# First block of a fused light convolution and feed-forward kernel: convolution work moved among TensorE, VectorE and GpSimd

## Chip, core and metric

One core of a Trainium2 chip runs the whole kernel. The metric is the time of one execution on the device in microseconds (us); for a kernel several runs are taken and their median is compared. All tensors are float32.

## What is computed

The input x has 8 sequences of 4096 tokens with 192 channels. A causal convolution comes first: for each of 8 heads (24 channels each) seven weights are put through a softmax, and each channel of a token is the weighted sum of that channel in this token and the six before it. Then a feed-forward layer follows:

```
w = softmax(weight, over the 7 taps)                # 8 heads x 7
y[t, c] = sum over k of w[head(c), k] * x[t - 6 + k, c]   # zero before a sequence
h = y @ w_in                                        # 192 -> 2048
g = h if h >= 1, 0 if h <= -1, else (h + 1)^2 / 4
out = g @ w_out                                     # 2048 -> 192
```

## The kernel before, in words

The 32768 tokens are cut into 64 blocks of 512. A block has 8 steps, one for each pair of 128-wide tiles of the 2048 hidden features; there are 512 steps, numbered q. In step q TensorE computes the hidden tiles (`mm1`, L351) and then the output matmuls of step q - 2 (`mm2_first`, L373, in the first two blocks; `mm2`, L395, after). Other engines turn h into g in between. Two PSUM buffers hold h, so `mm1` of step q + 2 needs h of step q to be read.

Block 0 runs `mm1` in plain float32: 6 products a step, each against halves of 64 partitions. From block 1 on, weights and activations are split into a rounded part and what is left, and `mm1` makes 18 matmuls of the faster rounded type (float32r). Its operands come in the order n (channels as they lie), s (halves swapped by DMA) and r (the channels from 128).

The order of the work on each engine is written out by hand; an engine takes its instructions in the order of the program, and each waits on what it needs.

Two blocks form a chunk of tokens, A and B. A unit of convolution is `a` (channels 0 to 127 of A), `b` (the same of B) or `r` (channels 128 to 191 of A and of B, one below the other). A unit is loaded in pieces of 32 channels and transposed by VectorE (`transpose`, L131), or, at the start, loaded with tokens on the partitions (`load_plain`, L101) and transposed by TensorE (`transpose_pe`, L133). Its seven taps are multiplied and summed on VectorE (`taps_dve`, L178), on ScalarE and GpSimd (`taps`, L188: ScalarE multiplies, GpSimd adds, L196 and L197), or by TensorE with diagonal matrices (`taps_pe`, L152). `split` (L206) makes the rounded part on ScalarE and the rest of it on VectorE or GpSimd, and swaps the halves of both by four DMAs of the SP queue (L202, L203).

The weights w_in and w_out come in ten chunks as pairs of words. ScalarE scales both words (`floats`, L286: m and r), VectorE puts them together (`bits`, L297: L304, L306 and L311 or L313). Later ScalarE rounds them (`hi`, L328) and VectorE makes the rest (`lo`, L332); the tables `PARTS` (L643) say in which step.

The start (L531 to L610): a few matmuls on dummy data, the loads on SP, the softmax of the weights, a matmul (`spread`, L578) that hands each channel its weights. Unit a takes taps 4 to 6 on VectorE and 0 to 3 on TensorE; unit r takes all seven on VectorE. Then the words of chunks 0, 1 and half of 2 are turned, and step 0 can begin.

`first_step` (L659) is the work of ScalarE and VectorE in steps 0 to 7: relu and square on ScalarE (L669, L675), the maximum on VectorE (L679), the words of chunk q + 3, the taps of unit b on VectorE by the table `FIRST_B` (L619), and in step 6 the split of unit b, ahead of the square. `conv_slot` (L623) starts the units of the next chunk. `evac_last` (L477) adds the output sums of the last block, transposes them with matmuls (L497) and stores them.

Of the kernel before, what the change touches and what calls it, by code (L numbers as in the profile page):

```python
# [30 lines left out]
def lightconv_then_ffn(ctx: ExitStack, tc: tile.TileContext, x, weight, w_in, w_out, out):  # L31
# [52 lines left out]
    def load_raw(t0s, chans, engs=None):  # L84


        raw = xin.tile([P, NG, SQ], F32, name="raw")
        first = [t0 % S == 0 for t0 in t0s]
        for i0 in (0, 2):
            if first[i0]:  # L90
                nc.gpsimd.memset(raw[i0 * SQ:(i0 + 2) * SQ, 0, :], 0.0)
        for i in range(4):
            lo = 1 if first[i] else 0
            src = xf[t0s[i] - SQ + lo * SQ:t0s[i] + TB, chans[i]:chans[i] + SQ]
            (engs[i] if engs else nc.sync).dma_start(
                out=raw[i * SQ:(i + 1) * SQ, lo:, :],
                in_=src.rearrange("(j a) b -> a j b", a=SQ),
            )
        return raw

    def load_plain(eng, c0, n, *t0s):  # L101

        raw = xin.tile([P, NG, SQ], F32, name="raw").rearrange("p j b -> p (j b)")[:, 0:TB]
        to = raw.rearrange("p (t i c) -> p t i c", t=TB // P, i=len(t0s))
        for i, t0 in enumerate(t0s):
            eng.dma_start(out=to[:, :, i], in_=xf[t0:t0 + TB, c0:c0 + n].rearrange(
                "(t p) c -> p t c", p=P))
        return raw

    def load_unit(c, u, engs=None):  # L110
        ta, tb = 2 * c * TB, (2 * c + 1) * TB
        if u == "r":
# [8 lines left out]
    class Conv:  # L121


        def __init__(self, c, u, raw):
            self.c, self.u, self.raw = c, u, raw
            self.wsel = 1 if u == "r" else 0

        def transpose(self):
            self.xT = xw.tile([P, NG * SQ], F32, name="xT")
            self.y = xw.tile([P, TB], F32, name="y")  # L130
            nc.vector.transpose(out=self.xT, in_=self.raw.rearrange("p j b -> p (j b)"))  # L131

# [18 lines left out]

        def taps_pe(self, banks, ks):  # L152

# [3 lines left out]
            for k in (*ks, None):  # L157
                for half, y in zip(HALVES, self.ys):
                    if k is None:
                        nc.tensor.matmul(y, ident[half], self.y[half], start=False, stop=True)  # L160
                    else:
                        nc.tensor.matmul(y, diags[half, k, :], self.xT[half, SH + k:SH + k + TB],
                                         start=(k == ks[0]), stop=False)

        def keep_pe(self):
# [8 lines left out]
            for i, y in enumerate(self.ys):  # L174
                nc.scalar.copy(t[i], y)
            o["n"], o["s"] = (t[0][TOP], t[1][BOT]), (t[1][TOP], t[0][BOT])

        def taps_dve(self, *ks, first=0):  # L178
            y = self.y
            for k in ks:  # L180
                tap, wt = self.xT[:, SH + k:SH + k + TB], wk[:, self.wsel, k:k + 1]
# [5 lines left out]

        def taps(self, *ks):  # L188
            y = self.y
            for k in ks:  # L190
                tap, wt = self.xT[:, SH + k:SH + k + TB], wk[:, self.wsel, k:k + 1]
                if k == 0:
                    nc.scalar.mul(y, tap, wt)
                else:
                    p = xw.tile([P, TB], F32, name="p", bufs=3)
                    nc.scalar.mul(p, tap, wt)  # L196
                    nc.gpsimd.tensor_add(y, y, p)  # L197
# [20 lines left out]
        def both_pe(self, bank):  # L218

            self.ys = [ps_o.tile([P, TB], F32, name=bank)]  # L220
            nc.tensor.matmul(self.ys[0], ident[TOP], self.y[TOP], start=True, stop=True)

        def split_rest(self):
# [5 lines left out]
            for key, t in (("hi", hi), ("lo", lo)):  # L229
                w = self.swapped(t, "r" + key, 2)  # L230
                if self.c > 0:
                    xop[2 * self.c]["r", key] = (t[TOP], w[BOT])
                xop[2 * self.c + 1]["r", key] = (w[TOP], t[BOT])

# [105 lines left out]
    def mm1(q):  # L340

        s, j = divmod(q, NPAIR)
        h = hs[q] = ps_h.tile([P, 2, TB], F32, name="h")
        if s == 0:
            mms = [(WI[j], u, xop[s][u]) for u in "nsr"]
        else:
            mms = [(W[j][:, part], u, xop[s][u, x]) for u in "nsr"
                   for part, x in ((0, "hi"), (1, "hi"), (0, "lo"))]
        for n, (w, u, x) in enumerate(mms):
            for e in range(2):  # L350
                nc.tensor.matmul(h[:, e, :], w[HALVES[e], COL[u][e]:COL[u][e] + P], x[e],  # L351
# [125 lines left out]
    def evac_last(s):  # L477

# [5 lines left out]
        for a in "rm":  # L484
            u, v = part[a] = [ob.tile([P, TB], F32, name="t", bufs=4) for _ in range(2)]
# [4 lines left out]
        ps = [ps_h.tile([P, 2, TB], F32, name="h") for _ in range(2)]  # L490
        y = [ob.tile([P, TB], F32, name="sum") for _ in range(2)]
        for b in range(TB // P):
            i, e, n = b // 2, b % 2, slice(b * P, (b + 1) * P)
            for a, i_n, c in (("r", ident[:, 0:DR], slice(P, D)), ("m", plain, slice(0, P))):
                ts = part[a][i:]
                for t in ts:
                    nc.tensor.matmul(ps[e][:, i, c], t[:, n], i_n, start=(t is ts[0]),  # L497
                                     stop=(t is ts[-1]))
            to = y[i][:, e * D:(e + 1) * D]
            if e == 0:  # L500
                nc.scalar.copy(to, ps[e][:, i, 0:D])
            else:
                nc.vector.tensor_copy(out=to, in_=ps[e][:, i, 0:D])
            (nc.scalar if b == 2 else nc.sync).dma_start(
                out=out[s * TB + b * P:s * TB + (b + 1) * P], in_=to)
# [9 lines left out]
    nought = nought.bitcast(BF16)  # L515
    ident = const.tile([P, P], F32, name="ident")

    diags = ob.tile([P, 4, P], F32, name="t", bufs=4)

    def make_diags():  # L520
        for k in range(4):
            nc.scalar.mul(diags[:, k, :], ident, wk[:, 0, k:k + 1])
# [14 lines left out]
    raw_a = load_plain(nc.sync, 0, P, 0)  # L537
    raw_r = load_plain(nc.sync, P, DR, 0, TB)
    chunks[0].load(nc.sync)
    for n in range(1, 5):  # L540
        if n == 3:
            raw_b = load_unit(0, "b")
# [5 lines left out]
    for sel, c0, reps in ((0, 0, 1), (1, P, 2)):  # L548
# [9 lines left out]
    conv_a, conv_r, conv_b = (Conv(0, u, raw) for u, raw in  # L558
                              (("a", raw_a), ("r", raw_r), ("b", raw_b)))
    for u in (conv_a, conv_r):  # L560
        u.room()
    xT_ar = ps_h.tile([P, 2, TB], F32, name="h")
    tail_r = ps_h.tile([P, 2, TB], F32, name="h")[:, 0]
    conv_a.transpose_pe(xT_ar[:, 0])
# [6 lines left out]
    conv_a.fetch()  # L571
# [4 lines left out]
    spread = ps_o.tile([P, TB], F32, name="accr1")  # L576
    for sel in range(2):
        nc.tensor.matmul(spread[:, sel * K:(sel + 1) * K], whose[:, sel, :], heads,  # L578
                         start=True, stop=True)
    nc.vector.tensor_copy(out=wk, in_=spread[:, 0:2 * K].rearrange("p (s k) -> p s k", s=2))  # L580
# [9 lines left out]
    idle_matmuls(2)  # L590
    conv_r.transpose_pe(xT_ar[:, 1])


    conv_r.tail_pe(TB - P - DR, tail_r[:, 0:K - 1])
    make_diags()
# [177 lines left out]
```

## Time and profile before

| quantity | value |
|---|---|
| median of 3 runs | 2262.6 us (2261.68 to 2263.47) |
| the profiled execution, its own time | 2263.13 us |
| its span, first to last instruction | 2261.3 us |
| TensorE busy | 2253.2 us, 100% |
| VectorE busy | 2110.2 us, 93% |
| ScalarE busy | 1694.2 us, 75% |
| GpSimd busy | 1160.5 us, 51% |
| mean granted TensorE clock | 0.999 |

In the profile PE is TensorE, PEld its weight loads, DVE VectorE, ACT ScalarE, POOL GpSimd and SP the engine that issues most DMAs. PEclk is the granted TensorE clock, 1.00 for 2.4 GHz. An engine's busy share is a mean over stages with different limits: the steps after the first 50 us are all alike for TensorE, and the change concerns the first 50 us and the last 10.

### The profile page before, as it was taken

The page shows a single profiled execution, that of the slowest core. Times are in us where ns is not written, and L with a number is a line of the kernel's source. Part 1 is how long each engine was busy: PE and PEld are TensorE (multiplying, and loading weights), DVE is VectorE, ACT ScalarE, POOL GpSimd, SP SyncE. Part 2 cuts the span into 40 slices and gives each one's busy share as a digit, 9 for nine tenths or more (in the row PEclk, how much of TensorE's full clock was granted, in tenths as well). Part 3 has the DMA queues.
Part 4 walks back from the last instruction along what each step waited for, and adds up shares of the span by engine and source line. Part 5 has one row for each costly group of instructions (what it writes and reads, how often), then busy time and mean ns, then how long its engine had stood idle before and what let it go on. Part 6 is the DMA issues. An engine that isn't in the chain of part 4 may idle for free.

```text
span 2261.3 us, 48195 instructions
## 1 busy us (share of the span) xinstructions
PE 2253.2 (100%) x19676; PEld 2096.3 (93%) x19676; DVE 2110.2 (93%) x1862; ACT 1694.2 (75%) x2141; POOL 1160.5 (51%) x846
## 2 busy tenths in 40 slices
PE   9999999999999999999999999999999999999999
PEld 6999999999999999999999999999999999999998
DVE  8899999999999999999999999999999999999997
ACT  6678777778777777777877777877777777787775
POOL 0446544466445565455654446644556545565451
PEclk9999999999999999999999999999999999999999
DMA  7221222222222222222122222222222222212211
GB/s 160 49 51 36 48 49 49 51 47 42 46 46 51 53 39 51 49 46 53 36 49 48 49 51 48 42 46 46 50 53 39 51 49 46 54 36 49 48 34 24
DMA packets 441852, 110.94 MB, mean 49 GB/s; under 512 B 410144, under 2 KB 417312, under 8 KB 441632
## 3 DMA queue, kind: packets, MB, share of 16 engines
q1 hardware_dynamic: 441472, 107.77, 25.8%
q8 instruction: 155, 2.54, 0.5%
q14 instruction: 65, 0.53, 0.1%
q10 hardware_dynamic: 160, 0.10, 0.0%
HBM read 32.83 MB, written 25.17 MB: 26 GB/s over the span
## 4 chain that ended last, share of the span: by engine, by line
PE 99%; DVE 0%; ACT 0%; issue 0%; POOL 0%; POOLq 0%; DVEq 0%
PE h L351 47%; PE accm L395 30%; PE accr L395 20%; PE accm L373 1%; PE accr L373 1%; DVE y L185 0%; PE h L497 0%; PE accm L529 0%; DVE g L679 0%; ACT g L669 0%; DVE y L183 0%; PE h L137 0%; PE accr L578 0%; DVE gh L311 0%; DVE wa L306 0%
## 5 line engine op out<-in xcount | busy, mean ns | idle before, releaser
L197 POOL TENSOR_TENSOR y<-y,p 128x512 f32<-128x512 f32 x558 | 779.9, 1398 | 794.2 <-DVE g L417 559.8
L430 DVE TENSOR_TENSOR gl<-g,gh 128x1024 fp32r<-128x1024 f32 (+1 forms) x497 | 734.0, 1477 | 27.2 <-ACT gh L424 22.7
L412 ACT ACTIVATE g<-g 128x1024 f32<-128x1024 f32 (+1 forms) x505 | 535.3, 1060 | 242.9 <-DVE g L406 234.2
L424 ACT CAST gh<-g 128x1024 fp32r<-128x1024 f32 (+1 forms) x497 | 521.6, 1050 | 239.4 <-DVE g L417 229.1
L406 DVE TENSOR_SCALAR g<-h 128x1024 f32<-128x1024 f32 (+1 forms) x505 | 610.0, 1208 | 94.7 <-PE h L351 86.4
L351 PE MATMUL h<-hi,w 64*128 64x512 f32 x4032 | 653.6, 389 | 0.0
L417 DVE TENSOR_TENSOR g<-h,g 128x1024 f32<-128x1024 f32 (+1 forms) x505 | 613.8, 1216 | 9.8 <-ACT g L412 2.4
L395 PE MATMUL accm<-gh,w 64*128 64x512 f32 x3968 | 548.1, 388 | 0.0
L351 PEld LDWEIGHTS h<-hi,w 64*128 64x128 f32 x4032 | 431.6, 184 | 29.1
L395 PEld LDWEIGHTS accm<-gh,w 64*128 64x128 f32 x3968 | 425.1, 184 | 28.9
L351 PE MATMUL h<-lo,w 64*128 64x512 f32 x2016 | 421.4, 388 | 0.0
L196 ACT ACTIVATE p<-xT,wk 128x512 f32<-128x512 f32 x558 | 372.1, 709 | 0.2 <-POOL y L197 0.2
L395 PE MATMUL accr<-gl,wr 64*128 64x512 f32 x1984 | 321.0, 388 | 0.0
L395 PE MATMUL accr<-gh,wr 64*128 64x512 f32 x1984 | 321.0, 388 | 0.0
L395 PE MATMUL accm<-gl,w 64*128 64x512 f32 x1984 | 321.0, 388 | 0.0
L351 PE MATMUL h<-rhi,w 64*128 64x512 f32 x1008 | 310.9, 388 | 0.0
L351 PE MATMUL h<-rh,w 64*128 64x512 f32 x1008 | 310.9, 388 | 0.0
L351 PEld LDWEIGHTS h<-lo,w 64*128 64x128 f32 x2016 | 216.0, 184 | 14.7
L443 POOL TENSOR_TENSOR sum<-t 128x512 f32<-128x512 f32 (+1 forms) x126 | 162.8, 1313 | 128.5 <-ACT t L442 128.5
L395 PEld LDWEIGHTS accr<-gl,wr 64*128 64x128 f32 x1984 | 212.6, 184 | 14.6 <-DVE gl L430 0.2
L395 PEld LDWEIGHTS accm<-gl,w 64*128 64x128 f32 x1984 | 212.6, 184 | 14.5
L395 PEld LDWEIGHTS accr<-gh,wr 64*128 64x128 f32 x1984 | 212.6, 184 | 14.5
(114 smaller groups left out, 1939.9 us busy)
## 6 DMA issues: line engine op xcount, KB each, us to landing
out_dram<-osb SPq DMA_DIRECT2D x366, 64.0 KB, 2.0
raw<-in_x_dram SPq DMA_DIRECT2D x334, 68.0 KB, 2.4
hi<-hi SPq DMA_DIRECT2D x126, 128.0 KB, 2.4
lo<-lo SPq DMA_DIRECT2D x126, 128.0 KB, 2.3
rhi<-rh SPq DMA_DIRECT2D x64, 128.0 KB, 2.3
rlo<-rl SPq DMA_DIRECT2D x64, 128.0 KB, 2.4
words<-in_moe_w_in_dram SPq DMA_DIRECT2D x16, 192.0 KB, 4.2
words<-in_moe_w_out_dram SPq DMA_DIRECT2D x8, 384.0 KB, 4.2
```

The lines of the kernel that those rows point to most:

```text
L196: nc.scalar.mul(p, tap, wt)
L197: nc.gpsimd.tensor_add(y, y, p)
L351: nc.tensor.matmul(h[:, e, :], w[HALVES[e], COL[u][e]:COL[u][e] + P], x[e], start=(n == 0), stop=(n == len(mms) - 1))
L373: nc.tensor.matmul(accs[s][a, i][:, c0:c0 + D], g[half, e, b * P:(b + 1) * P], w[half, e, :], start=False, stop=(j == NPAIR - 1 and e == 1 ...
L395: nc.tensor.matmul(accs[s][a, i], st, g[HALVES[i], e, :], start=(j == 0 and n == first[a]), stop=(j == NPAIR - 1 and n == last[a]))
L406: nc.vector.tensor_scalar(out=g[:, e, :], in0=hs[q][:, e, :], scalar1=-1.0, scalar2=1.0, op0=ALU.max, op1=ALU.min)
L412: nc.scalar.activation(g[:, e, :], g[:, e, :], AF.Square, bias=0.5, scale=0.5)
L417: nc.vector.tensor_tensor(out=g[:, e, :], in0=h[:, e, :], in1=g[:, e, :], op=ALU.max)
L424: nc.scalar.copy(gh[:, e, :], gs[q][:, e, :])
L430: eng.tensor_sub(gl[:, e, :], g[:, e, :], gh[:, e, :])
L443: nc.gpsimd.tensor_add(y[:, n], t[0][:, n], t[1][:, n])
```

## The change

- Unit r of the first chunk becomes two units. For A, TensorE makes all seven taps: the lower 64 partitions hold the channels one token later (`late`), so that one full-height matmul with a diagonal matrix adds two taps. For B a new unit `rb`, 256 tokens above 256 tokens, is loaded, transposed and summed on VectorE in steps 2 to 5 and swapped by three DMAs each (`split_halves`): those of the rounded part from SP, those of the rest from ScalarE.
- Unit a of A takes taps 1 to 6 on VectorE and tap 0 on TensorE.
- Unit b: tap 0 on ScalarE, tap 1 on VectorE, taps 2 to 6 on ScalarE and GpSimd. A GpSimd sum follows a memset of GpSimd that follows a memset of VectorE to the same cell, just ahead of the maximum. Its split moves from within step 6 to that step's end.
- The words of chunk 2 are turned before and in step 0; from step 2 on a step turns chunk q + 2 in place of q + 3. Chunks 0 and 1 are rounded a step later.
- Step 0 works on its two halves by different ways; block 0's first products pair n with s, so that one copied tile serves two.
- `evac_last` adds both halves on VectorE, and transposes the sum with one matmul where two were.

The diff, cut to its core:

```diff
-    def load_plain(eng, c0, n, *t0s):
+    def load_plain(eng, c0, n, late=False):
...
+        eng.dma_start(out=to[:, :, 0], in_=x[0:TB].rearrange("(t p) c -> p t c", p=P))
+        if late:
+            nc.vector.memset(to[0:1, 0, 1], 0.0)
+            eng.dma_start(out=to[1:P, 0, 1], in_=x[0:P - 1])
+            eng.dma_start(out=to[:, 1:, 1],
+                          in_=x[P - 1:TB - 1].rearrange("(t p) c -> p t c", p=P))
...
+        def pairs_pe(self, bank, *ks):
+            if ks[0] == 1:
+                self.ys = [ps_o.tile([P, TB], F32, name=bank)]
+            for k in ks:
+                n = TOP if k == K - 1 else slice(0, P)
+                nc.tensor.matmul(self.ys[0], diag(self.u, k)[n], self.xT[n, SH + k:SH + k + TB],
+                                 start=(k == 1), stop=(k == K - 1))
...
-            for i, y in enumerate(self.ys):
-                nc.scalar.copy(t[i], y)
+            nc.scalar.copy(t[0], self.ys[0])
+            nc.vector.tensor_copy(out=t[1], in_=self.ys[1])
...
+        def split_halves(self):
+            n = self.n
+            y, late = self.y[:, 0:n], slice(n, TB)
...
+            for key, t, eng in (("hi", hi, nc.sync), ("lo", lo, nc.scalar)):
+                if t is hi:
+                    nc.scalar.copy(t[:, 0:n], y)
+                else:
+                    nc.vector.tensor_sub(t[:, 0:n], y, hi[:, 0:n].bitcast(F32))
...
+                for to, half in ((t32[TOP, late], BOT), (w32[BOT, late], BOT),
+                                 (w32[BOT, 0:n], TOP)):
+                    eng.dma_start(out=to, in_=t32[half, 0:n])
...
+                yield
...
-            mms = [(WI[j], u, xop[s][u]) for u in "nsr"]
+            mms = [(WI[j], us, [xop[s][u] for u in us]) for us in ("ns", "sn", "rr")]
...
-            nc.vector.tensor_copy(out=v[:, half], in_=acc[a, 1][:, half])
-            nc.vector.tensor_tensor(out=v[:, rest], in0=acc[a, 1][:, rest], in1=u[:, rest],
-                                    op=ALU.add)
+            for n in (half, rest):
+                nc.vector.tensor_tensor(out=v[:, n], in0=acc[a, 1][:, n], in1=u[:, n], op=ALU.add)
...
-    spread = ps_o.tile([P, TB], F32, name="accr1")
...
+    spread = [ps_o.tile([P, TB], F32, name=f"accr{1 - sel}") for sel in range(2)]
...
+    nc.vector.tensor_copy(out=wk[:, 0], in_=spread[0][:, 0:K])
+    nc.scalar.copy(wk2[TOP], spread[1][TOP, 0:K])
+    nc.scalar.copy(wk2[BOT, 1:], spread[1][BOT, 0:K - 1])
+    make_diag("a", 0)
+    make_diag("r", 1)
+    idle_matmuls(1)
+    conv_r.transpose_pe(xT_1[:, 0])
+    conv_r.fetch(xT_1[:, 0])
+    for k in (3, 5, K - 1):
+        make_diag("r", k)
+    nc.scalar.copy(wk[:, 1], spread[1][:, 0:K])
...
-    conv_a.taps_dve(4, 5, 6, first=4)
-    conv_a.taps_pe(("accm0", "accm1"), range(4))
...
-    conv_r.taps_dve(*range(K))
...
+    conv_a.taps_dve(*range(1, K), first=1)
+    conv_a.tap_pe(("accm0", "accm1"), 0)
+    conv_r.pairs_pe("accr0", 1, 3, 5)
+    conv_a.join_pe()
+    conv_r.pairs_pe("accr0", K - 1)
...
-    FIRST_B = {1: (0, 1), 2: (2,), 3: (3, 4), 4: (5,), 5: (6,)}
+    FIRST_B = {2: 2, 3: 3, 4: 4, 5: 5, 6: 6}
+    FIRST_RB = {3: (0, 1), 4: (2, 3), 5: (4, 5, 6)}
...
-        PARTS[5 + j].append((j, False))
+        PARTS[5 + j if j > 1 else 6 + j].append((j, False))
...
     def first_step(q):
-        n = q + LAG + 1
+        n = q + LAG
...
+        a, f, b = both_square(q, g), chunks[n].floats(), chunks[n].bits()
+        advance(a, f)
+        if q == 2:
+            conv_b.taps(0)
+        k = FIRST_B.get(q)
+        p = conv_b.product(k) if k else None
+        advance(a)
+        if q < 6:
+            advance(b)
+        if k:
+            nc.vector.memset(warm, 0.0)
+            nc.gpsimd.memset(warm, 0.0)
+            nc.gpsimd.tensor_add(conv_b.y, conv_b.y, p)
+        most(hs.pop(q), g)
+        advance(f)
+        if q < 6:
+            advance(b)
+        if q == 2:
+            conv_rb.transpose()
+            conv_b.taps_dve(1)
+        conv_rb.taps_dve(*FIRST_RB.get(q, ()))
+        if q == 5:
+            splits.append(conv_rb.split_halves())
+        if splits and q < 7:
+            next(splits[0])
+        parts_hi(q + 1)
+        parts_lo(q)
         if q == 6:
             conv_b.split(nc.vector)
...
+        if q >= 6:
+            advance(b, b)
```

## Rows read from the trace of the kernel before

**Rows 1.** The page, engines: busy us (share of the span) x instructions.

```profile
PE 2253.2 (100%) x19676; PEld 2096.3 (93%) x19676; DVE 2110.2 (93%) x1862; ACT 1694.2 (75%) x2141; POOL 1160.5 (51%) x846
```

**Rows 2.** Stretches: length, busy us of each engine (x instructions), PEclk, DMA, GB/s.

```profile
11.43:13.80 2.37, 0.00 (x1) 0.00 (x0) 2.30 (x4) 1.07 (x2) 0.00 (x0) 1.00 1.26 164
15.46:19.40 3.94, 3.94 (x11) 1.95 (x13) 3.35 (x8) 1.87 (x5) 0.00 (x0) 0.57 1.07 257
19.40:23.00 3.60, 3.18 (x16) 1.32 (x12) 1.81 (x4) 2.96 (x6) 0.00 (x0) 1.00 0.85 201
28.88:54.72 25.84, 25.84 (x222) 19.65 (x221) 23.71 (x38) 19.23 (x27) 0.00 (x0) 1.00 0.66 140
```

**Rows 3.** The chain that ended last, 0 to 55 us: start, us, what.

```profile
6.17 0.50 DVE y L183
...
6.69 0.76 DVE y L185
...
15.46 4.56 PE h L351 x12
...
23.11 2.85 PE h L351 x12
...
28.88 2.58 PE h L351 x12
...
54.72 2.11 PE h L351 x18
```

**Rows 4.** Timeline of the start: start, us, engine, line, operation, [idle before].

```profile
5.14 0.59 ACT L150 COPY xT<-h 128x512 f32<-128x512 f32 x1 [2.10 <-PE h L137]
...
6.16 1.28 ACT L522 ACTIVATE t<-ident,wk 128x128 f32<-128x128 f32 x4 [0.43 <-DVE wk L580]
...
6.87 3.70 PE L162 MATMUL accm<-xT,t 64*128 64x512 f32 x16
...
13.66 0.35 DVE L304 TENSOR_SCALAR wa<-m 128x384 uint32<-128x384 uint32 x1
...
15.42 0.36 DVE L304 TENSOR_SCALAR wa<-m 128x384 uint32<-128x384 uint32 x1
```

**Rows 5.** Timeline of step 4 on VectorE.

```profile
36.62 0.55 DVE L304 TENSOR_SCALAR wa<-m 128x768 uint32<-128x768 uint32 x1
...
37.21 0.96 DVE L306 SCALAR_TENSOR_TENSOR wa<-m,wa 128x768 uint32<-128x768 uint32 x1
...
39.53 0.55 DVE L311 CUSTOM_DVE_ANT_0 gl<-wa,r 128x768 uint16<-128x768 uint16 x1
...
40.47 1.22 DVE L679 SCALAR_TENSOR_TENSOR g<-g,h 128x1024 f32<-128x1024 f32 x1
```

**Rows 6.** Timeline of steps 5 and 6, ScalarE and SP; last the page's DMA issues.

```profile
41.84 1.03 ACT L669 ACTIVATE g<-h 128x1024 f32<-128x1024 f32 x1 [1.16 <-PE h L351]
...
44.96 0.51 ACT L328 CAST w<-gh 128x384 fp32r<-128x384 f32 x1
...
48.51 0.62 ACT L211 CAST hi<-y 128x512 fp32r<-128x512 f32 x1 [0.46 <-DVE y L185]
...
49.67 0.59 SPq L203 DMA_DIRECT2D hi<-hi  x1
...
hi<-hi SPq DMA_DIRECT2D x126, 128.0 KB, 2.4
```

**Rows 7.** Timeline of step 9: GpSimd additions and a VectorE subtraction beside them.

```profile
61.42 2.83 POOL L197 TENSOR_TENSOR y<-y,p 128x512 f32<-128x512 f32 x2 [56.66 <-ACT p L196]
...
63.02 1.37 DVE L332 TENSOR_TENSOR wr<-wf,wr 128x128 fp32r<-128x128 f32 x1
```

**Rows 8.** Timeline of the end.

```profile
2255.46 0.42 DVE L488 TENSOR_TENSOR t<-accm,t 128x256 f32<-128x256 f32 x1
...
2258.03 0.38 ACTq L504 DMA_DIRECT2D out_dram<-sum  x1
2258.35 0.36 DVE L503 COPY sum<-h 128x192 f32<-128x192 f32 x1 [0.80 <-PE h L497]
```

More of the change, by code (lines that the diff above doesn't have):

```diff
@@ L491, in evac_last @@
-        y = [ob.tile([P, TB], F32, name="sum") for _ in range(2)]
[L492 to L505, printed above, removed]
+            for n in (half, rest):
+                nc.vector.tensor_tensor(out=v[:, n], in0=acc[a, 1][:, n], in1=u[:, n], op=ALU.add)
@@ new lines, in evac_last @@
+            part[a] = v
+        ps = [ps_h.tile([P, 2, TB], F32, name="h")[:, 0] for _ in range(2)]
+        ps += [ps_o.tile([P, TB], F32, name=f"accr{i}") for i in range(2)]
+        y = [ob.tile([P, TB], F32, name="sum") for _ in range(2)]
+        for i in range(2):
+            for b in (2 * i, 2 * i + 1):
+                nc.tensor.matmul(ps[b][:, P:D], part["r"][:, b * P:(b + 1) * P], ident[:, 0:DR],
+                                 start=True, stop=True)
+            for b in (2 * i, 2 * i + 1):
+                nc.tensor.transpose(ps[b][:, 0:P], part["m"][:, b * P:(b + 1) * P], plain)
+            for b, copy in ((2 * i, nc.scalar.copy), (2 * i + 1, nc.vector.tensor_copy)):
+                copy(y[i][:, b % 2 * D:(b % 2 + 1) * D], ps[b][:, 0:D])
+                if i == 1:
+                    (nc.sync if b % 2 else nc.scalar).dma_start(
+                        out=out[s * TB + b * P:s * TB + (b + 1) * P],
+                        in_=y[i][:, b % 2 * D:(b % 2 + 1) * D])
+            if i == 0:
+                nc.sync.dma_start(
+                    out=out[s * TB:s * TB + 2 * P].rearrange("(b p) d -> p b d", p=P),
+                    in_=y[i][:, 0:2 * D].rearrange("p (b d) -> p b d", b=2))
@@ L536, in lightconv_then_ffn @@
     nc.scalar.dma_start(out=heads, in_=weight)
[L537 to L542, printed above, removed]
+    raw_a = load_plain(nc.sync, 0, P)
+    raw_r = load_plain(nc.sync, P, DR, late=True)
+    for n in range(3):
         chunks[n].load(nc.sync)
@@ L588, in whole @@
             pass
[L590 to L595, printed above, removed]
-    conv_a.taps_dve(4, 5, 6, first=4)
-    conv_a.taps_pe(("accm0", "accm1"), range(4))
-    conv_r.fetch()
-    nc.vector.tensor_copy(out=conv_r.xT[BOT, SH:SQ], in_=tail_r[BOT, 0:K - 1])
-    conv_r.taps_dve(*range(K))
+    conv_a.taps_dve(*range(1, K), first=1)
[3 more added lines that the diff above has]
+    conv_r.pairs_pe("accr0", K - 1)
     floats(0)
-    floats(1)
+    chunks[3].load(nc.sync)
+    raw_b = load_unit(0, "b")
+    f1 = chunks[1].floats()
+    next(f1)
     whole(0)
+    conv_a.keep_pe()
+    next(f1)
+    chunks[4].load(nc.sync)
+    raw_rb = load_unit(0, "rb")
+    conv_b, conv_rb = Conv(0, "b", raw_b), Conv(0, "rb", raw_rb)
     whole(1)
-    conv_r.both_pe("accr0")
-    conv_a.keep_pe()
     conv_r.keep_pe()
@@ L654, in parts_lo, with advance, both_square, most @@
             chunks[n].lo(rest)
-    bits = {LAG: chunks[LAG].bits(CI)}
-    next(bits[LAG])
+    def advance(*steps):
+        for i in steps:
+            next(i)
+    def both_square(q, g):
+        h = hs[q]
+        nc.scalar.activation(g, h, AF.Relu, bias=0.5, scale=0.5)
+        yield
+        nc.scalar.activation(g, g, AF.Square)
+        yield
+    def most(h, g, e=slice(0, 2)):
+        nc.vector.scalar_tensor_tensor(out=g[:, e], in0=g[:, e], scalar=1.0, in1=h[:, e],
+                                       op0=ALU.min, op1=ALU.max)
@@ L670, in first_step @@
+        parts_hi(q + 1)
+        parts_lo(q)
         if q == 6:
             conv_b.split(nc.vector)
-        if n - 1 in words:
-            next(words.pop(n - 1))
-        for e in ts:
-            nc.scalar.activation(g[:, e], g[:, e], AF.Square)
-        def most():
-            for e in ts:
-                nc.vector.scalar_tensor_tensor(out=g[:, e], in0=g[:, e], scalar=1.0, in1=h[:, e],
-                                               op0=ALU.min, op1=ALU.max)
-        if q == 0:
-            most()
@@ L700, in first_step @@
         conv_slot(q, conv_b, conv_n.get("a"), conv_n.get("r"))
-    words = {}
     conv_n = {}
```

163 lines of the change are left out of this document (87 added, 76 removed).

## Prediction

> **What bounds the kernel now.** I read the page's busy shares first: TensorE is busy all of the span [rows 1], so time can be won only where TensorE stands still or its clock is low, ahead of the long even stretch and behind it. The table by stretches, over the head, shows where: it is idle for 2.37 us, then a stretch at a granted clock of 0.57 follows, that is, mostly at 1.2 GHz, and from 28.88 us to 54.72 us it is busy throughout [rows 2]. The chain of waits gives the marks [rows 3]: the hidden matmuls (L351) of steps 0, 2 and 3 begin at 15.46, 23.11 and 28.88, those of step 8, the first of the second token block, at 54.72. Before 15.46 the chain is on VectorE's taps. Step 2 takes 28.88 - 23.11 = 5.77; steps 3 to 7 take (54.72 - 28.88) / 5 = 5.17 each; the L351 part of a step 2.58. What is won before 28.88 counts only if step 8 is not kept waiting, as the change moves work towards it.
>
> **The head.** VectorE's taps of the remaining channels leave the front (7 of them), and those of channels 0 to 127 grow from three to six. They can start when the transposed copy is there, 5.14 + 0.59 = 5.73 [rows 4], since the weights now come by a bank of their own and before the 6.17 of today; six taps are 0.52 + 5 x 0.77 = 4.4 [rows 3], done at 10.2. On TensorE 16 records, 8 half-height matmuls (four pairs), took 3.70 [rows 4]; in L351 three pairs take 2.58, 0.86 a pair. A full-height matmul of the same width is not in the trace of before: from half a pair's time (0.43) to a pair's at half clock (1.7); I take 0.86, the same columns at the same clock. So tap 0 of the first channels runs from about 6.9 to 7.8, after the rest's transposes. The first paired matmul then writes the bank accr0, in which the second spread lies, and that is last read by ScalarE's copy into wk[:, 1], behind two small copies, five diagonals of 1.28 / 4 = 0.32 each and the fetch (0.59): about 8.6. Three pairs from 8.6 end at 11.2, the two joining matmuls at 12.1, the last tap at 13.0. Only then comes step 0's L351: **13.0 in place of 15.46**. The words are turned in time (VectorE is done with chunk 0 at 11.9, a group of 384 columns taking 15.42 - 13.66 = 1.76 [rows 4]). With no long idle TensorE should keep 2.4 GHz. Steps 0 and 1 take 2 x 2.58, a wait for step 0's result 0.2, step 2 5.77: step 3 begins at 24.1, **4.8 earlier**. Chunk 2's copies and the second vector operation of step 0 lie beside L351 of step 1; without that cover they would cost about 1.8. SP's queue gains one load ahead of the words (0.5 each); ScalarE reads the first words only near 8.6, so that costs nothing.
>
> **Steps 2 to 6.** Tap 1 and all of the rest of block B stay on VectorE; taps 2 to 6 of B go to GpSimd. That takes five taps of 0.75 off VectorE, 3.8, and puts on it seven taps of 256 columns. A tap of that width is not in the trace; half of 0.77 and the whole of it are the ends, I take 0.3 for the first and 0.5 for the others, as a fixed part stays: 3.3. Nor is a GpSimd addition beside these VectorE instructions there. The nearest rows: two additions took 2.83 together, and a VectorE subtraction of 128 columns that started beside them took 1.37 and ended with them [rows 7], while a two-input instruction over 384 columns takes 0.55 with GpSimd still [rows 5]. The additions are released just ahead of the maximum (1.22, reading PSUM), so about 0.35 of each sticks out and holds the next VectorE instruction; the ends are 0 and 1.4. Hence VectorE is no freer than before. From 5.8 it has to do, up to the rest's last tap in step 5: taps 4.4; six groups of 384 columns 10.6; one PSUM copy and three half-wide operations in step 0 at a little over half a maximum, 2.7; five maxima 5.7, at 1.22 less the some 0.08 by which neighbours overlap (two of 0.55 fill 0.94 [rows 5]); two transposes and tap 1, an estimate from the tap's 0.77, 1.9; chunks 4 to 7 at 0.59 + 0.90 + 0.94 = 2.4 each [rows 5], 9.7; seven short taps 3.3; four holds and memsets 1.7. Sum 40.0: **the last tap ends at 45.8**, with hardly a gap.
>
> **Step 6, where the head's gain is tested.** Step 8's L351 could begin at 24.1 + 25.84 = 49.9. It needs block B: the rounded y, what is left of it, and both with halves swapped by SP. Before, that split stood early in step 6 (copy at 48.51 [rows 6]) and had until 54.72. Now it stands at the end of step 6, behind on ScalarE: the copy of the rest (it waits for the last tap: 46.2), a cast (0.4), step 6's relu, words, product and square (1.0, 0.5, 0.6, 1.0; the square ends at 49.7), then, after VectorE's maximum and subtraction (51.4), three DMA issues, two casts and the split's copy. TensorE's step 6 ends L351 at 42.2, so step 6's relu starts some 4.4 late. A DMA issue by ScalarE took 0.38 [rows 8]; how long it holds up the ScalarE work behind it no row shows plainly, so it is bounded by 0 and by the 0.59 of SP's issue [rows 6]; I take 0.38. The copy then ends at 54.05. With SP's second issue (0.59) and 2.4 to land [rows 6] the swapped half is there at 57.0, the last of the four transfers at 58.2, and after the third operand (0.7) step 8's L351 ends at 59.1. Before, it ended at 54.72 + 2.11 = 56.83. So the **4.8 are given back and 2.3 more**. TensorE is idle for over 4 us there, more than the 2.37 that were followed by the clock of 0.57 [rows 2]; L351 of step 0 lost up to 4.56 - 2.58 = 2.0 to that. Much of step 8's L351 waits for transfers anyway, so I take 0.7, from 0 to 2.0. Casts of chunks 0 and 1 come one step later; they are ready before the swapped half and hide behind it.
>
> The Trainium skill, DMA: Bandwidth & Descriptors, Issuing engines are not separate DMA queues, says that starting DMAs from several engines saves no more than sequencer time, which is usually small beside the DMA. By that the three ScalarE issues would buy no faster transfer; read as costing ScalarE nothing, they would make the net 1.1 less than mine. The row's 0.38 is a sixth of the 2.4 to landing, which speaks for a small cost, but three of them stand in line.
>
> **The end.** Both halves of the last sums are added on VectorE, and each quarter then needs one matmul a part in place of two for the first two quarters. Today the sums are added up to 2255.46 + 0.42 for the first half [rows 8], and the last copy starts at 2258.35. After: the second half's addition ends at 2256.3, eight matmuls and transposes follow in four banks, and the last copy starts near 2257.5. The gain is 0.9, from 0 (if the added VectorE work is the path) to 1.3.
>
> **Sum.** +2.3 + 0.7 - 0.9 = +2.1. The profiled execution took 2263.13 (span 2261.3 and 1.8 around it), 0.5 above the median of 2262.6; I add to the median: **2264.7**. About 0.2%, 4.5 us, is what a measurement of this kernel can tell from no change, so this forecast is "within".
>
> **Rivals.**
> - No stall at step 8. If VectorE and ScalarE keep up, the gain is 4.8 + 0.9 = 5.7: 2256.9, faster. For it: VectorE's load by step is near TensorE's 5.17, and small errors add up over 40 us. Against: VectorE is already busy for 23.71 of 25.84 [rows 2].
> - Stall without the lag. Step 6's relu starts on time at 42.2; the same line of ScalarE work brings the last transfer at 53.8, and L351 of step 8 ends at 54.7, 2.1 earlier than before: with the end 2259.6, within. It needs holds near 0 and shorter taps.
> - Slower: the low clock lasts. At step 8 TensorE restarts in pieces between transfers. If it stays at 1.2 GHz through that L351 and the output matmuls behind it (2.11 + 2.59 of work, doubled; 2.59 is 5.17 - 2.58), 4.7 take the place of 0.7: 2268.7. It decides once more than 3.1 us of work run at half speed (then the net passes +4.5). Against: before, the clock was back at 19.40, 3.9 after the restart. Dearer ScalarE issues (0.59) add 0.6 to it.
> - The change does not do what it says: the diagonals and the shared bank delay the paired matmuls so far that TensorE's head wins little. That is in the 8.6 above; 1 us more would come off the 4.8, but step 8 is bound by VectorE, and nothing more is lost. I give it no chance of its own.
>
> **How the numbers follow.** Forecast 0.52 (2262 to 2267), stall without lag 0.18, no stall 0.18, low clock 0.12. Faster by over 0.2% is the no-stall case, 0.18; slower the last, 0.12; within 0.70. The range goes from 2256.8, which takes in half of the no-stall case, to 2267.5 (2264.7 with 0.6 for dearer issues, 1.3 for the clock and 0.9 for a VectorE sum 2% longer): some 0.17 is left out.
>
> **What would show it.** Right: L351 of step 0 near 13.0 and of step 3 near 24; a granted clock of 1.0 up to 40 us; VectorE nearly without gaps to 45; ScalarE's relu of step 6 behind the rest's copy; L351 of step 8 starting near 54 with TensorE idle from 50, and waiting for the swapped halves. Wrong: L351 of step 8 starting at 50 to 51, VectorE gaps in steps 3 to 5, or a first paired matmul that starts at 7.8.

## The result, and the profile after

The changed kernel takes 2267.07 us (median of 14 runs, 2265.81 to 2269.64), the kernel before 2262.68 in the same comparison: the ratio is 1.0021, with a 95% interval from 1.0013 to 1.0028. It is 4.4 us slower. That is 0.19% by the medians and 0.21% by the ratio, on the edge of the 0.2% which the prediction called no change, and clearly not equal. Forecast was +2.1, half of that, in a range that holds the measured time. The profiled execution after has a span of 2265.0, 3.7 more than that of before; the rest of the 4.4 lies in where the two profiled executions stand among their own runs (0.5 above the median before, 0.35 below it after, at 2266.72). Of 31 runs of the kernel before, taken beside the first experiments, 13 took 2261.68 to 2261.80 at a mean granted clock of 1.000 and 18 took 2262.34 to 2263.50 at 0.999; the profiled one is of the second kind, so the low clock at its start may not stand in every run.

The page of the changed kernel, engines, answers to [rows 1]: TensorE is still busy all of the span, so this line shows nothing of the loss.

```profile
PE 2255.4 (100%) x19655; PEld 1926.4 (85%) x19655; DVE 2109.2 (93%) x1869; ACT 1697.5 (75%) x2151; POOL 1169.4 (52%) x856
```

The chain that ended last, of the changed kernel (start, us, what), answers to [rows 3]. `mm1` is now L385.

```profile
9.58 2.81 PE accr L177 x6
...
14.31 2.69 PE h L385 x11
...
54.02 0.53 ACT hi L229
54.56 2.17 DMA hi<-hi
...
56.78 3.93 PE h L385 x11
...
63.48 2.03 PE h L385 x17
```

Step 0 begins 1.15 earlier by the chain (14.31 against 15.46), and as it meets no low clock, step 3 begins 3.3 earlier (25.39 in the timeline below, against 28.68 in the timeline of before, whose chain has 28.88). Step 9 begins 4.08 later by the chain (63.48; in the chain of before 59.40). Between them the chain leaves TensorE: it goes to ScalarE's copy of block B's split (L229) and to the DMA that swaps its halves.

The table by stretches (length, busy us of PE, PEld, DVE, ACT and POOL with their instructions, PEclk, DMA share, GB/s), which answers to [rows 2], shows the price in TensorE's terms.

```profile
28.40:49.90 21.50, 21.50 (x190) 15.85 (x188) 17.46 (x32) 16.39 (x22) 6.29 (x9) 1.00 0.60 124
51.43:54.59 3.16, 0.00 (x1) 0.00 (x1) 0.26 (x2) 1.50 (x4) 0.00 (x0) 0.91 0.28 62
54.59:56.70 2.11, 1.65 (x6) 0.79 (x6) 2.04 (x4) 2.11 (x3) 0.00 (x0) 0.50 0.48 105
56.70:58.80 2.10, 2.02 (x7) 1.12 (x7) 1.92 (x4) 1.00 (x3) 0.00 (x0) 0.50 0.66 144
58.80:60.20 1.40, 1.40 (x9) 1.10 (x10) 1.23 (x4) 0.00 (x0) 0.00 (x0) 0.50 0.04 12
...
60.00:61.50 1.50, 1.50 (x15) 1.40 (x15) 1.45 (x3) 0.00 (x0) 0.00 (x0) 0.72 0.00 0
```

TensorE stands still for 3.16 us ahead of step 8, which the kernel before never did there, and then works at a granted clock of 0.50 (1.2 GHz) until 60.2 at least; it is 0.72 on the mean from 60.0 to 61.5 and 1.00 (2.4 GHz) from there on.

The timeline of the changed kernel's start, which answers to [rows 4]:

```profile
8.98 0.15 ACT L628 COPY wk<-accr 128x7 f32<-128x7 f32 x1
...
9.51 0.34 PEld L177 LDWEIGHTS accr<-xT,t 128*128 128x128 f32 x2 [1.50 <-ACT wk L628]
9.51 2.88 PE L177 MATMUL accr<-xT,t 128*128 128x512 f32 x6
...
13.53 0.69 DVE L190 COPY hi<-accm 128x512 f32<-128x512 f32 x1 [1.60 <-PE accm L168]
...
14.13 1.98 PE L385 MATMUL h<-hi,gh 64*128 64x512 f32 x8
...
25.39 1.88 PE L385 MATMUL h<-hi,gh 64*128 64x512 f32 x8
```

The first paired matmul (L177) follows ScalarE's copy of the weights (L628), as its bank had to be read off. VectorE then has a gap of 1.60 for the joining matmul. The timeline of steps 5 to 8, which answers to [rows 5, 6]:

```profile
43.13 0.81 DVE L343 CUSTOM_DVE_ANT_0 gl<-wa,r 128x768 uint16<-128x768 uint16 x1
...
44.33 1.51 DVE L201 SCALAR_TENSOR_TENSOR y<-xT,wk,y 128x256 f32<-128x256 f32 x3
...
45.88 0.40 ACT L256 CAST rh<-y 128x256 fp32r<-128x256 f32 x1 [3.17 <-DVE warm L771]
...
46.60 1.02 ACT L712 ACTIVATE g<-h 128x1024 f32<-128x1024 f32 x1
...
49.65 1.22 DVE L719 SCALAR_TENSOR_TENSOR g<-g,h 128x1024 f32<-128x1024 f32 x1 [3.79 <-ACT g L714]
...
50.79 0.42 DVE L258 TENSOR_TENSOR rl<-y,rh 128x256 fp32r<-128x256 f32 x1
...
51.24 0.53 ACTq L263 DMA_DIRECT2D rl<-rl  x1
51.80 1.25 ACTq L263 DMA_DIRECT2D rlo<-rl  x2
53.09 0.92 ACT L360 CAST w<-gh 128x384 fp32r<-128x384 f32 x2 [3.02 <-issue]
53.92 0.61 ACT L229 CAST hi<-y 128x512 fp32r<-128x512 f32 x1
...
54.59 1.22 PE L385 MATMUL h<-hi,w 64*128 64x512 f32 x4 [3.16 <-ACT hi L229]
...
58.74 0.28 PEld L385 LDWEIGHTS h<-lo,w 64*128 64x128 f32 x1 [0.38 <-DMA lo<-lo]
...
60.19 0.62 PE L385 MATMUL h<-rlo,w 64*128 64x512 f32 x1
```

Read it down ScalarE's column: the copy of the rest (L256) waits 3.17 for VectorE's last short tap; the relu of step 6 (L712) stands behind it; VectorE's maximum (L719) then waits 3.79 for ScalarE's square; the remainder (L258) follows it; three DMA issues follow the remainder; two casts follow them; and only then comes the copy of the split, on which TensorE waits. The last of the four swaps (`lo`) is there at 58.74, and step 8's hidden matmuls end at 60.19 + 0.62 = 60.81.

The end, timeline, answers to [rows 8]:

```profile
2258.80 0.40 PE L429 MATMUL accm<-gl,w 64*128 64x512 f32 x2
...
2261.48 0.36 DVE L533 COPY sum<-accr 128x192 f32<-128x192 f32 x1 [0.26 <-PE accr L531]
```

From the end of the last sum (2259.20; before 2254.42 + 0.40 = 2254.82) to the end of the span it is 5.8 us, before 6.5: the new end gains 0.7.

So, between the two traces: 3.3 won at the head and kept up to step 6; at the end of step 9's hidden matmuls it stands at +4.0 (chain, 63.48 + 2.03 = 65.51 against 59.40 + 2.11 = 61.51), so some 7.3 were lost at step 8. The chain is 4.1 behind from step 18 on and stays so until the last step. There 0.3 more is lost, between VectorE's last product (L451; before L417) and ScalarE's rounding of it (L458; before L424), and then 0.7 is won: 3.7. First the row of before, then that of the changed kernel:

```profile
2251.07 1.17 ACT L424 CAST gh<-g 128x512 fp32r<-128x512 f32 x2 [1.16 <-DVE g L417]
...
2255.45 1.14 ACT L458 CAST gh<-g 128x512 fp32r<-128x512 f32 x2 [1.44 <-DVE g L451]
```

That idle time is 1.43 to 1.44 in three of the fourteen profiles and 1.15 to 1.16 in the others, nine of which have the changed kernel's end steps too. So these 0.3 are put down to the execution and not to the change; why they arise is open.

### The profile page after: what moved, and what is told of

Read it like the earlier page. It is cut to its first block, busy times and chain, and to the rows that moved or that the text cites. A ratio compares the mean times of both kernels' runs of the same rounds, so it can differ in the third digit from the quotient of the medians.

```text
span 2265.0 us, 48197 instructions
## 1 busy us (share of the span) xinstructions
PE 2255.4 (100%) x19655; PEld 1926.4 (85%) x19655; DVE 2109.2 (93%) x1869; ACT 1697.5 (75%) x2151; POOL 1169.4 (52%) x856
## 4 chain that ended last, share of the span: by engine, by line
PE 98%; DVE 1%; ACT 0%; issue 0%; DMA 0%; ACTq 0%; SPq 0%; POOL 0%; POOLq 0%; DVEq 0%
PE h L385 46%; PE accm L429 30%; PE accr L429 20%; PE accr L407 1%; PE accm L407 1%; DMA words<-in_moe_w_out_dram 0%; PE accr L177 0%; PE accm L571 0%; DVE gl L343 0%; DVE y L201 0%; DMA hi<-hi 0%; PE accm L162 0%; ACT g L714 0%; DVE wf L345 0%; PE h L147 0%
## 5 line engine op out<-in xcount | busy, mean ns | idle before, releaser
L385 PE MATMUL h<-hi,w 64*128 64x512 f32 x4032 | 769.2, 389 | 3.7 <-ACT hi L229 3.2
L446 ACT ACTIVATE g<-g 128x1024 f32<-128x1024 f32 (+1 forms) x505 | 535.3, 1060 | 245.9 <-DVE g L440 237.3
L458 ACT CAST gh<-g 128x1024 fp32r<-128x1024 f32 (+1 forms) x497 | 521.6, 1050 | 238.0 <-DVE g L451 225.0
L429 PE MATMUL accm<-gh,w 64*128 64x512 f32 x3968 | 640.5, 388 | 0.0
L385 PEld LDWEIGHTS h<-hi,w 64*128 64x128 f32 x4032 | 569.9, 185 | 69.4 <-ACT hi L229 3.5
L451 DVE TENSOR_TENSOR g<-h,g 128x1024 f32<-128x1024 f32 (+1 forms) x505 | 613.8, 1216 | 10.2 <-ACT g L446 2.8
L385 PE MATMUL h<-lo,w 64*128 64x512 f32 x2016 | 610.4, 389 | 0.0
L429 PE MATMUL accr<-gh,wr 64*128 64x512 f32 x1984 | 413.6, 388 | 0.0
L429 PE MATMUL accr<-gl,wr 64*128 64x512 f32 x1984 | 413.5, 388 | 0.0
L429 PE MATMUL accm<-gl,w 64*128 64x512 f32 x1984 | 413.4, 388 | 0.0
L385 PEld LDWEIGHTS h<-lo,w 64*128 64x128 f32 x2016 | 371.8, 185 | 33.3 <-DMA lo<-lo 0.5
L385 PE MATMUL h<-rh,w 64*128 64x512 f32 x1008 | 311.5, 389 | 0.0
L385 PE MATMUL h<-rhi,w 64*128 64x512 f32 x1008 | 311.3, 388 | 0.0
L429 PEld LDWEIGHTS accr<-gl,wr 64*128 64x128 f32 x1984 | 280.2, 184 | 32.5 <-DVE gl L464 0.5
L429 PEld LDWEIGHTS accr<-gh,wr 64*128 64x128 f32 x1984 | 280.2, 184 | 32.1
```

The costliest lines, as they stand in the source:

```text
L385: nc.tensor.matmul(h[:, e, :], w[HALVES[e], c0:c0 + P], x[e][e], start=(n == 0), stop=(n == len(mms) - 1))
L429: nc.tensor.matmul(accs[s][a, i], st, g[HALVES[i], e, :], start=(j == 0 and n == first[a]), stop=(j == NPAIR - 1 and n == last[a]))
L446: nc.scalar.activation(g[:, e, :], g[:, e, :], AF.Square, bias=0.5, scale=0.5)
L451: nc.vector.tensor_tensor(out=g[:, e, :], in0=h[:, e, :], in1=g[:, e, :], op=ALU.max)
L458: nc.scalar.copy(gh[:, e, :], gs[q][:, e, :])
```

## The experiments

Theory A: step 8 waits because the split of block B stands at the end of a queue on ScalarE. Rival B: GpSimd's sums and VectorE hold each other up. Rival C: the low clock is the main loss. A fourth, D, came up on the way. All times are medians, each beside the kernel before on the same chip; the changed kernel is taken from the result above. The intervals of the edits that bring under 2 us overlap with its own (1.0013 to 1.0028), so what these edits do is read from their traces. One thing there differs from execution to execution: with the same code at the start, step 0 begins at 13.27 to 14.82 in nine profiles.

**The split ahead of remainder and casts (split_first).**

```diff
+        if q == 6:
+            conv_b.split(nc.vector)
         if splits and q < 7:
             next(splits[0])
         parts_hi(q + 1)
         parts_lo(q)
-        if q == 6:
-            conv_b.split(nc.vector)
```

> Only the place of block B's split changes: in step 6 it stands ahead of the rest's remainder, its three ScalarE DMAs and the casts. Theory A (step 8 waits for the split behind those): the copy of the split starts near 50.1 in place of 53.9, the swapped halves land near 53.7 to 54.8, the hidden matmuls of step 8 end near 56 in place of 60.7, and the whole is 4 to 5 us faster than the changed kernel, about 2262.5. Theory B (the loss is GpSimd and VectorE holding each other up in steps 2 to 5): step 8 is bound by the same late work, 1 us at most is won, about 2266. Theory C (the loss is mostly the low clock at step 8): the pause becomes shorter but not short, the granted clock is still 0.5 there, about 2264.

Measured 2265.41, 1.7 faster than the changed kernel, ratio to the kernel before 1.0013 (1.0004 to 1.0023). At step 8 theory A holds: the split's copy starts at 49.54 (4.4 earlier, of which 0.6 is the earlier start of this execution), step 8's last hidden matmul ends at 56.2, and no low clock follows. But the gain is not kept. The chain of this run, steps 9 to 11, and TensorE's waits (engine, line, awaited: us, times, longest):

```profile
61.90 1.07 ACT g L446
...
66.01 1.06 ACT g L446
67.07 0.36 ACT t L475
...
68.63 0.32 PE accr L401
...
71.50 2.13 PE h L385 x18
```

```profile
PE h L385 <- DVE g L451: 0.9, 1, 0.9
PE accm L401 <- ACT t L475: 0.8, 1, 0.8
```

ScalarE's square (L446) runs late, the copies that empty block 0's sums (L475) stand behind it, and TensorE's first output matmuls of block 1 (L401), in step 10, wait for them. Step 11 begins at 71.50, after the change at 73.19, before at 69.10. The cure moved the wait two steps on.

**The remainder by SP (lo_by_sp).**

```diff
-            for key, t, eng in (("hi", hi, nc.sync), ("lo", lo, nc.scalar)):
+            for key, t, eng in (("hi", hi, nc.sync), ("lo", lo, nc.sync)):
```

> Only the queue of three DMAs changes: the rest's remainder goes out by SP in place of ScalarE. Theory A: ScalarE is freed of 1.8 us, the split's copy starts near 51.1, but its swaps stand behind the three on SP and land 0.8 to 1.5 us earlier than now; about 2266. If a DMA issue cost ScalarE nothing, the split's copy would stay at 53.9 and the time at 2267. Theory B: no change, 2267.

Measured 2265.75, 1.3 faster; ratio 1.0014 (1.0005 to 1.0023). Its timeline:

```profile
50.93 0.62 ACT L229 CAST hi<-y 128x512 fp32r<-128x512 f32 x1
...
55.50 1.86 PE L385 MATMUL h<-hi,w 64*128 64x512 f32 x4 [2.53 <-DMA hi<-hi]
```

The split's copy starts at 50.93, 3.0 earlier, which shows that the three issues, with the wait for the remainder ahead of them, do hold up ScalarE. The swaps then stand behind the three on SP, and TensorE waits 2.5 us for the swapped half. So the sum is as theory A has it.

**The copy of the rest a step later (rb_copy_late).**

```diff
+        if q == 6:
+            next(splits[0])
         most(hs.pop(q), g)
...
-        if splits and q < 7:
+        if q == 6:
             next(splits[0])
```

> Only the place of one ScalarE copy changes: the rounded copy of the rest of block B goes from the end of step 5 to step 6, behind the square. Theory A (that copy waits for VectorE's last short tap and keeps step 6's relu back): relu of step 6 starts near 43.7 in place of 46.6, the split's copy near 51.2 in place of 53.9, and the whole is 2.5 to 3 us faster, about 2264.3. Theory B: VectorE's lateness stays and something else waits for it, 2267. Theory C: the low clock stays, 2265 to 2266.

Measured 2265.75, ratio 1.0011 (1.0001 to 1.0021): 1.3 faster where 2.5 to 3 was expected. Relu of step 6 starts at 44.40, the split's copy at 52.00: 2.2 and 1.9 earlier. The low clock stays (granted 0.50 from 57 to 60, 0.67 from 60 to 63). Half the expected size: step 8's hidden matmuls end 1.9 earlier (58.89 against 60.81), but step 9's start only 0.4 earlier (62.57 against 62.97), as the clock is low through more of the output matmuls between them. This execution also started late (step 0 at 14.82, 0.7 after that of the changed kernel).

**Both moves (both_moves).** The two edits above together, the remainder still by ScalarE.

> The copy of the rest goes behind the square of step 6 and the split of block B ahead of the remainder and the casts. Theory A: the split's copy starts near 47.7, the swapped halves land near 51.2 to 52.3, the hidden matmuls of step 8 start near 51.2, with hardly a stall and no low clock; the 3.3 us of the head and the 0.7 of the end are kept: about 2259, faster than the kernel before by 3 to 4 us. Theory B: step 8 still starts near 53 or later, 2264 or more. Theory C does not differ from A here, as no pause is left.

Measured 2262.89, ratio 1.0003 (0.9994 to 1.0013): as the kernel before, not 3 to 4 us faster. Step 8 begins at 51.52 with the clock at 1.00, as expected. What was not: step 7. Its timeline:

```profile
49.48 0.54 ACTq L263 DMA_DIRECT2D rl<-rl  x1
...
52.38 1.02 ACT L712 ACTIVATE g<-h 128x1024 f32<-128x1024 f32 x1
...
54.80 1.22 DVE L719 SCALAR_TENSOR_TENSOR g<-g,h 128x1024 f32<-128x1024 f32 x1 [3.44 <-ACT g L714]
```

TensorE had h of step 7 ready at 49.2; relu starts at 52.38, behind the DMA issues and two casts; VectorE stands still for 3.44 us, and is late into step 10, where L401 again waits 0.8. Hence theory D: what counts is VectorE's backlog up to step 12.

**Both moves and SP (moves_sp).** The edits of both_moves and lo_by_sp.

> Both moves of step 6, and the rest's remainder sent by SP in place of ScalarE. In the run with both moves alone step 8 began early, but ScalarE's three DMA issues kept relu of step 7 back, VectorE stood still for 3.4 us and then ran late into steps 9 to 11, where TensorE waited 2 us again. Theory D (what decides is VectorE's backlog up to step 12, and that pause is what it lacks): relu of step 7 starts near 49.3 in place of 52.4, the wait at steps 10 and 11 goes, and the time is 2260.5 to 2261.5. Theory A (only the split's place decides): the remainder lands a little later behind the swaps, 2262.9 or 0.5 more.

Measured 2260.54, ratio 0.9993 (0.9984 to 1.0002): 6.5 faster than the changed kernel. The relu of step 7 comes at once, and TensorE's only wait between 50 and 110 us is the last of step 8:

```profile
49.29 1.02 ACT L712 ACTIVATE g<-h 128x1024 f32<-128x1024 f32 x1
...
51.76 1.22 DVE L719 SCALAR_TENSOR_TENSOR g<-g,h 128x1024 f32<-128x1024 f32 x1 [0.37 <-ACT g L714]
```

```profile
PE h L385 <- DMA rlo<-rl: 0.8, 1, 0.8
```

**The same pause, met by less work (moves_rests).** Both moves, remainder by ScalarE, and VectorE's remainders of the second weights three steps later:

```diff
-        PARTS[9 + j].append((j + LAG, True))
+        PARTS[12 + j].append((j + LAG, True))
```

> Both moves of step 6, and the remainders of the second weights (rest parts of chunks 2 to 9), which VectorE makes in steps 9 to 16, three steps later. Theory D (VectorE's backlog): steps 9 to 12 lose some 1.8 to 2.6 us of VectorE work each, TensorE's wait at steps 10 and 11 goes, 2260.5 to 2261.5. Theory A: no change against both moves alone, 2262.9.

Measured 2262.33, ratio 1.0001 (0.9992 to 1.0010). The wait of L401 is still 0.8. The 0.6 against both_moves is inside the intervals, and the two profiled executions differ by 1.0 (spans 2260.5 and 2261.5), as their heads do (step 0 at 13.55 against 14.53). So theory D falls as put: the wait does not go with the VectorE work of steps 9 to 12, but it goes with the pause in step 7 (moves_sp).

**The other bank (bank).**

```diff
-    conv_r.pairs_pe("accr0", 1, 3, 5)
+    conv_r.pairs_pe("accr1", 1, 3, 5)
...
-    conv_r.pairs_pe("accr0", K - 1)
+    conv_r.pairs_pe("accr1", K - 1)
```

> The changed kernel with the paired matmuls in the other bank (accr1), read off early by VectorE, so that they need not wait for ScalarE's late copy of the second spread. If the shared bank delays the head: the first paired matmul starts when TensorE is free, up to 0.8 earlier, and step 0's hidden matmuls some 0.5 to 0.8 earlier. Theory D (VectorE sets step 8): the whole is within 0.3 us of the changed kernel all the same, 2267. If the head's gain carried through: 2266.2.

Measured 2265.89, ratio 1.0018 (1.0009 to 1.0026): 1.2 faster than the changed kernel, where I had put 0.3 at most. From its timeline:

```profile
8.08 2.84 PE L177 MATMUL accr<-xT,t 128*128 128x512 f32 x6
...
12.66 1.98 PE L385 MATMUL h<-hi,gh 64*128 64x512 f32 x8
...
44.41 0.40 ACT L256 CAST rh<-y 128x256 fp32r<-128x256 f32 x1 [3.16 <-DVE warm L771]
```

The first paired matmul starts 1.43 earlier than after the change (9.51) and no longer waits for the copy; the other two marks are 1.47 earlier (14.13 and 45.88). The three profiles with this bank have step 0 at 12.48 to 12.94, below all nine of the others, so the head's gain is clear, while the 1.2 of the whole is not clear of noise (4 of its 11 runs lie below all those of the changed kernel). VectorE is not gapless in the head: it waits there for TensorE's joining matmul, so the head is a stretch of its own and what is won in it moves all that follows.

**The clock held up (keep_clock).** The changed kernel with 15 matmuls of zeros into step 8's hidden buffer, ahead of its own.

```diff
+        if q == NPAIR:
+            for _ in range(15):
+                nc.tensor.matmul(h[:, 0, :], nought[:, 0:P], nought[:, 0:TB],
+                                 start=True, stop=True)
```

> The changed kernel with 15 matmuls of zeros into the hidden buffer of step 8 ahead of that step's own, in the 3.2 us in which TensorE stands still; they add no data. Theory C (the low clock is a large part of the loss): the granted clock stays 1.0 through step 8, and 1.3 to 1.6 us of the 4.4 are won back, about 2265.6. Theory A (the wait is the loss, the clock a small addition, as step 8's matmuls wait for transfers anyway): 0.7 us, about 2266.4. If the zeros don't hold the clock: 2267.

Measured 2267.33, ratio 1.0023 (1.0014 to 1.0032): no gain. The stretches (columns as above):

```profile
50.70:54.70 4.00, 3.42 (x17) 1.49 (x17) 0.34 (x2) 1.71 (x4) 0.00 (x0) 1.00 0.25 53
54.70:56.80 2.10, 1.14 (x7) 0.40 (x5) 1.87 (x5) 2.10 (x4) 0.00 (x0) 1.00 0.55 121
...
58.80:60.30 1.50, 1.50 (x12) 1.37 (x14) 1.33 (x4) 0.00 (x0) 0.00 (x0) 0.71 0.00 0
60.30:63.00 2.70, 2.70 (x21) 2.70 (x20) 2.43 (x4) 0.70 (x1) 0.00 (x0) 0.53 0.00 0
```

The zeros keep the clock at 1.00 through the pause, but in step 8 itself TensorE waits for transfers again, and the clock falls behind that, in the output matmuls. The price was moved, not saved. Step 8's hidden matmuls end at 60.05 in place of 60.8, step 9's begin 0.6 later. One more thing differs: this execution started 0.9 earlier and still made the split's copy only 0.1 earlier, as the third DMA issue of ScalarE took 1.37 (51.58 to 52.95) in place of 0.6. So the price of the clock alone is not separated by this run.

**Without GpSimd (no_gpsimd).** Taps 2 to 6 of block B on VectorE, no products on ScalarE.

```diff
-        p = conv_b.product(k) if k else None
+        p = None
...
-            nc.vector.memset(warm, 0.0)
-            nc.gpsimd.memset(warm, 0.0)
-            nc.gpsimd.tensor_add(conv_b.y, conv_b.y, p)
+            conv_b.taps_dve(k)
```

> The changed kernel with taps 2 to 6 of block B on VectorE again, at the place of the two memsets and the GpSimd sum, and without ScalarE's products. Theory A: VectorE gains 5 taps of 0.75 and loses holds of about 0.25 and memsets: the last short tap of the rest comes 1.5 to 2 us later than 45.8, step 8 as much later, about 2268.5. Theory B (the sums on GpSimd cost more than they bring): the same or faster, 2267 or less.

Measured 2267.95, ratio 1.0026 (1.0015 to 1.0036), 0.9 slower than the changed kernel. L343 takes 0.55 without GpSimd beside it, 0.81 with it: a hold of 0.26. The copy of the rest starts at 47.64, 1.8 later, as theory A had it; as ScalarE has no product in step 6, a third of that comes back (the split's copy starts at 55.08, 1.2 later). Rival B falls: without GpSimd's sums VectorE is later and not earlier. That the sums pay in the whole time is not clear of noise.

**The new end alone (old_with_new_end).** The kernel before with the new `evac_last`.

> The kernel before with the new end alone (both halves added by VectorE, one matmul a part and quarter). From the traces the stretch from the last sum to the end of the span is 5.8 us with the new end and 6.5 with the old one: 0.5 to 0.8 us faster than the kernel before, about 2262.0. If the end's gain is lost in the last store: no difference.

Measured 2262.09, ratio 0.9997 (0.9988 to 1.0005): 0.5 by the medians, inside the interval, and 5.8 from the last sum to the end in its trace as after the change.

**Both moves, SP and the other bank (moves_sp_bank, moves_pool_bank).** moves_sp with the other bank; then the same with the remainder by GpSimd's queue.

> Both moves of step 6, the remainder by SP, and the paired matmuls in the bank that is free early. In the run with the bank alone the whole chain, VectorE's too, came 1.4 us earlier and the time fell by 1.2. If the head is a stretch of its own ahead of a chain that keeps its length, that adds to the 2260.5 of both moves with SP: about 2259.2, over 3 us faster than the kernel before. If VectorE's backlog is the bound once the pause at step 8 is gone, TensorE waits again in steps 9 to 11 and the time stays near 2260.5.

> As the run before, but the rest's remainder goes out by GpSimd's queue, where nothing else stands in steps 6 and 7. TensorE's last wait of step 8 (0.8 us for that remainder, third in line on SP) should go if GpSimd's issue takes less than some 2 us: about 2258.5. If GpSimd takes longer to make the transfers, or the VectorE work beside it holds it up, 2259.2 or more.

Measured 2259.90 and 2259.88, both 0.9991 of the kernel before (0.9982 to 1.0000): 2.8 us faster than it by the medians, at the edge of what the interval tells apart, and 7.2 faster than the changed kernel, which is clear. In the first step 0 begins at 12.94, step 9 at 56.31, and no wait returns in steps 9 to 11; the bank brings 0.6 here by the medians (not clear of noise) and 1.6 between the two profiled spans (2258.0 and 2259.6). In the second the 0.8 for the remainder goes, but the swapped remainder of block B (lo) comes 0.7 late, and the time is the same. Steps 3 to 11 then run with a wait of under 1 us.

## Why the prediction was right, and where not

**The mechanism** was the one forecast: the head's gain is given back at step 8, by ScalarE's queue in step 6. Its marks, forecast and measured: last short tap 45.8 and 45.84; copy of the rest done 46.2 and 46.28; square done 49.7 and 49.6; remainder done 51.4 and 51.21; split's copy done 54.05 and 54.53; swapped half there 57.0 and 57.3 (SP's second issue at 55.07 and 2.2 to land); last transfer there 58.2 and 58.7. The size was not: +2.1 against +4.4, or +3.7 between the traces. lo_by_sp and rb_copy_late take one link out each and gain 1.3; all links out (moves_sp) gain 6.5.

**The head** was overrated: 4.8 forecast, 3.3 measured. The step that failed there is "three pairs from 8.6": the rest's transposes ended near 7.6 rather than 6.9, the diagonals took 0.33 to 0.40, and the pairs began at 9.51. I wrote of the shared bank that 1 us "would come off the 4.8, but step 8 is bound by VectorE, and nothing more is lost"; the bank run, in which all that follows is 1.47 earlier, speaks against it. VectorE's 40.0 us of work "with hardly a gap" came out at the right time by luck, as two errors cancel: it has a gap of 1.6 at the joining matmul, and the rest of the 39.9 from 5.94 to 45.84 is 38.3, 1.7 less than forecast. Of that 0.4 is in the four holds (0.26 each where I put 0.35); where the rest is was not taken apart. It is by this luck too that the head's miss did not reach the sum, since step 8 was reckoned from VectorE's 45.8 and not from the head.

**ScalarE's issues** were taken at 0.38 each; three took 51.24 to 53.05, 0.6 each, and the next ScalarE instruction starts at 53.09. The Trainium skill, DMA: Bandwidth & Descriptors, Issuing engines are not separate DMA queues, calls that time usually small beside the DMA. In this trace one issue is 0.6 beside 2.0 to land, and the three in line are 1.8 us on the path that ends last; lo_by_sp moves the split's copy by 3.0.

**The clock** was taken at 0.7. Step 8 ended at 60.8 in place of 59.1, 1.7 late. Of that 0.5 is the last transfer (58.7 in place of 58.2), which goes back to ScalarE's issues, dearer by 0.7. The seven matmuls behind it took 2.07 (58.74 to 60.81) at a granted 0.50; the same seven before ended at 56.83, their pair of `lo` starting at 55.72, that is 1.1 at 1.00:

```profile
55.72 0.42 PE L351 MATMUL h<-lo,w 64*128 64x512 f32 x2
```

So by this estimate about 1.0 is the clock, in place of 0.7 and within the ends of 0 and 2.0, and 0.2 is that the forecast allowed 0.9 for these seven. Split_first, where step 8 has no long pause, keeps 1.00. The low clock lasted through step 8 and ended at the output matmuls, so the rival in which it lasts through both fell; rb_copy_late, at 0.67 from 60 to 63, came nearer to it. With these sizes (2.3, 0.5, 0.2 and 1.0) step 8 ends 4.0 late; less 0.7 for the end in place of 0.9 that is +3.3, and the 0.1 behind step 9 and the 0.3 of the last step make the 3.7 of the trace.

**The end** gained 0.7 by the trace, forecast 0.9.

**The rivals.** "No stall" and "stall without the lag" fell; moves_sp shows what it is worth to have no long stall: 2.0 below the kernel before by the medians, where 5.7 had been put. Not foreseen at all: that step 8, once mended, hands the wait to step 10.

## What to carry to other kernels

Where one engine is busy throughout, work won ahead of its even stretch counts only if every queue behind it is as early; follow the last link of each later step by name before counting the gain. On an engine that works in order, the place of an instruction that waits (a copy for a late sum, a DMA issue for a late remainder) costs all that stands behind it: put it behind what others need next. After mending a wait, look for the next one in the same engines' queues; here single edits brought 1.3 to 1.7 of 6.5, and it took three together before the kernel was ahead of the old one by its median.

## What had not been expected of the hardware

A DMA issue by ScalarE held that engine for 0.53 to 0.62 us in the changed kernel, as long as SP's, though the engine's own work was ready; one of the three took longer in four other runs, 0.80 to 0.87 in rb_copy_late, both_moves and moves_rests and 1.37 in keep_clock, and why was not tried. And 15 matmuls of zeros held the granted clock at 1.00 for a pause of 4 us, but it fell to 0.53 afterwards, behind stretches in which TensorE was busy for 1.14 of 2.10 and 1.67 of 2.00 us.
